# A fused retention and MLP kernel on one core: step inputs in three transfers, y1 stores from ScalarE's queue

## The chip, the core and the metric

The kernel runs on one core of one Trainium2 chip. The metric is device time in microseconds of one execution. A core has five engines that run their own queues in order: TensorE (PE in the profile, PEld for its weight loads), VectorE (DVE), ScalarE (ACT), GpSimd (POOL) and SyncE (SP). In this kernel SyncE only issues DMA transfers; ScalarE issues three at the start. The queue that issues a transfer is named SPq or ACTq.

## What is computed

Three stages follow each other over 3072 tokens: a retention layer (8 heads, head size 64, 4 batches of 768 positions, a state that decays by gamma per position), a first MLP (512 to 1024 to 512, with h * softmax(h) and a layer norm between) and a second MLP (512 to 2048 to 512, with h * cos(h) between).

```python
for t in range(S):
    state = gamma[None, :, None, None] * state + np.einsum('bhd,bhe->bhde', k[:, :, t], v[:, :, t])
    y[:, :, t] = scale * np.einsum('bhd,bhde->bhe', q[:, :, t], state)
...
h = x @ w_in
solu = h * softmax(h)
ln = (solu - mu) / np.sqrt(var + 1e-06) * g_ln
x = ln @ w_out
...
h = x @ w_in
return ((h * np.cos(h)) @ w_out).astype(np.float32)
```

## The kernel before

**Retention in steps.** The positions are cut into chunks of 64. Two batches and all heads go together, so there are 24 steps, two runs of 12. load_step(n) (L83) loads a step's inputs, 1 MB: kt (k by head dimension, 256 KB, two buffers), X (q, two halves of 64 partitions), W (v, two halves of 64 partitions) and kn (k by position, 256 KB); X, W and kn have three buffers. That is six transfers (L91 to L98), all from SyncE. att_prep (L216) lets ScalarE scale kn in place (L223). att_scores multiplies kt and X on TensorE (L230, L231), and VectorE masks the product into the free halves of X (L248). att_state multiplies kn and W into the running state (L241), and ScalarE copies it into the free halves of the next step's W (L255, L256). att_out multiplies W and X to the step's y (L287), and VectorE scales it (L290). attend() (L457) does one round of it: it loads step n+2, prepares step n+1, computes the scores of n+1 and the state and output of n.

**First MLP.** mm1 (L315) multiplies with w1, norm (L318) is softmax and norm over VectorE, ScalarE and GpSimd, transp (L341) transposes the result on TensorE (L351) and splits it into a high part lth (ScalarE, L354) and a rest ltl (VectorE, L355), two buffers of tr. mm2 (L359) multiplies with w_out1; after two halves ScalarE copies the sum to ys (L372, one buffer), and SyncE stores it to y1d in DRAM (L373), 24 stores of 256 KB.

**Weights.** They come as 64-bit floats. load_w (L142) loads a raw tile of 512 KB (L155) into one of three buffers and converts it on ScalarE (L158) and VectorE (L161 to L167) to wt, two buffers. For the tiles that there is no room for yet, keep (L188) stores the converted tile of 256 KB to DRAM (L191), 28 of them; load_kept (L193) fetches them later, two at a time. The list wq (L442) holds all weight tiles, and weights(n) takes the next ones between the other work.

**Second MLP.** load_y (L376) reads y1d back, up (L385) and down (L409) are its two products (L393, L418).

**Order.** TensorE runs in the order of the program text (manual_schedule, L54). The order of every other queue, SyncE's among them, is drawn up by a planner that plays the program through on a timeline of its own (schedule_with_timeline_sim, L663); only single operations are held to program order. Each queue then runs in that order, and an instruction that waits holds up those behind it.

Of the kernel before, what the change touches and what calls it, by code (L numbers as in the profile page):

```python
# [11 lines left out]
F32 = mybir.dt.float32  # L12
# [35 lines left out]


@with_exitstack  # L50
def body(ctx: ExitStack, tc: tile.TileContext, qx, kt, kn, vn, c_sc, c_mg,
         w_in1, w_out1, gln, w_in2, w_out2, out):
    nc = tc.nc
    pe_order = tc.manual_schedule(engines={mybir.EngineType.PE})  # L54
# [28 lines left out]
    def load_step(n):  # L83
        bp, i = steps[n]
        d = {}
        d["kt"] = pa.tile([128, 8, C], F32, tag="kt", name="kt", bufs=2)
        d["X"] = pa.tile([128, 2, 8, C], F32, tag="X", name="X")
        d["kn"] = pa.tile([128, NHP, 2 * D], F32, tag="kn", name="kn")
        d["W"] = pa.tile([128, 2, 8, D], F32, tag="W", name="W")
        d["mg"] = pa.tile([128, 2, NHP, C], F32, tag="mg", name="mg", bufs=2)  # L90
        nc.sync.dma_start(out=d["kt"], in_=kt[bp, i].rearrange("p (j s) -> p j s", s=C))  # L91
        src = qx[bp, i].rearrange("p (j s) -> p j s", s=C)
        nc.sync.dma_start(out=d["X"][64:128, 0], in_=src[64:128])
        nc.sync.dma_start(out=d["X"][0:64, 1], in_=src[0:64])
        src = vn[bp, i].rearrange("p (j s) -> p j s", s=D)
        nc.sync.dma_start(out=d["W"][0:64, 0], in_=src[0:64])
        nc.sync.dma_start(out=d["W"][64:128, 1], in_=src[64:128])
        nc.sync.dma_start(out=d["kn"], in_=kn[bp, i].rearrange("p (j s) -> p j s", s=2 * D))  # L98
        if i == 0:
            nc.gpsimd.memset(d["W"][64:128, 0], 0.0)  # L100
            nc.gpsimd.memset(d["W"][0:64, 1], 0.0)
        st[n] = d

    load_step(0)
# [37 lines left out]
    def load_w(src, apart=False):  # L142
        seq[0] += 1
        if early:
            raw = early.pop(0)
            src = None
            t = p_boot.tile([128, 512], I32, tag="wt", name="wt", bufs=4)
        elif "lt" not in p2 and seq[0] % 2:
            raw = p2["boot"].tile([128, 512, 2], I32, tag="raw", name="raw", bufs=3)
            t = p2["boot"].tile([128, 512], I32, tag="wt", name="wt", bufs=2)  # L150
        else:
            raw = stg.tile([128, 512, 2], I32, tag="raw", name="raw", bufs=3)
            t = stg.tile([128, 512], I32, tag="wt", name="wt")
# [31 lines left out]
    w2h, w2l = {}, {}  # L185
    kept = {}

    def keep(kind, c, e, k, src):  # L188
        if k == 0:
            kept[kind, c, e] = dram.tile([128, 2, 512], F32, name=f"kept_{kind}_{c}_{e}")  # L190
        nc.sync.dma_start(out=kept[kind, c, e][:, k], in_=load_w(src))  # L191

    def load_kept(what, hi, lo):  # L193
        t = stg.tile([128, 2, 512], F32, tag="raw", name="raw", bufs=3)
# [30 lines left out]
    def score_pair(n, j):  # L225
        d = st[n]
        if j == 0:
            d["sc"] = psa.tile([128, 8, C], F32, tag="sc", name="sc")
        sc = d["sc"]
        nc.tensor.matmul(out=sc[0:64, j], lhsT=d["kt"][64:128, j], rhs=d["X"][64:128, 0, j], start=True, stop=True)  # L230
        nc.tensor.matmul(out=sc[64:128, j], lhsT=d["kt"][0:64, j], rhs=d["X"][0:64, 1, j], start=True, stop=True)  # L231

    def state_pair(n, j):
        i = steps[n][1]
        d = st[n]
        if i == 0 and j == 0:
            s_ps[0] = psa.tile([128, 8, D], F32, tag="S", name="S")
        sp = s_ps[0]
        k3 = d["kn"].rearrange("p a (b d) -> p (a b) d", b=2)
        for r, par in ((slice(0, 64), 0), (slice(64, 128), 1)):  # L240
            nc.tensor.matmul(out=sp[r, j], lhsT=k3[r, j], rhs=d["W"][r, par, j],  # L241
                             start=(i == 0 and j == 0), stop=(i == NI - 2 and j == 7), skip_group_check=True)

    def score_mask(n):
        d = st[n]
        sc = d["sc"]
        for r, par in ((slice(0, 64), 0), (slice(64, 128), 1)):
            nc.vector.tensor_tensor(  # L248
                out=d["X"][r, par].rearrange("p (a b) t -> p a b t", b=2),
                in0=sc[r].rearrange("p (a b) t -> p a b t", b=2),  # L250
                in1=d["mg"][r, 0].unsqueeze(2).to_broadcast([64, NHP, 2, C]), op=ALU.mult)

    def state_copy(n):
        nd, sp = st[n + 1], s_ps[0]
        nc.scalar.activation(out=nd["W"][64:128, 0], in_=sp[0:64], func=AF.Copy)  # L255
        nc.scalar.activation(out=nd["W"][0:64, 1], in_=sp[64:128], func=AF.Copy)  # L256

    def att_scores(n):
        for j in range(8):
# [22 lines left out]
    def att_out(n):  # L282
        d = st[n]
        y = psa.tile([128, 8, C], F32, tag="y", name="y")
        for j in range(8):
            for par in range(2):
                nc.tensor.matmul(out=y[64 * par:64 * par + 64, j], lhsT=d["W"][:, par, j], rhs=d["X"][:, par, j],  # L287
                                 start=True, stop=True)
# [70 lines left out]
    def mm2(g, p, e):  # L359
        if e == 0:  # L360
            y1s[g] = p2["pst"].tile([128, 2, 256], F32, tag="y1", name="y1")
        y1 = y1s[g]
        ds = slice((2 * p + e) * 128, (2 * p + e + 1) * 128)
        m = 0
        for j in range(K1):
            lh, ll = lt[g][j // 2]
            for w, a in ((o1[0], lh), (o1[1], lh), (o1[0], ll)):
                nc.tensor.matmul(out=y1[:, e], lhsT=w[:, j, ds], rhs=a[:, j % 2], start=(m == 0), stop=(m == 3 * K1 - 1))  # L368
                m += 1
        if e == 1:  # L370
            ys = moe.tile([128, 2, 256], F32, tag="ys", name="ys", bufs=1)
            nc.scalar.activation(out=ys, in_=y1, func=AF.Copy)  # L372
            nc.sync.dma_start(out=y1d[g // 2][:, 2 * p:2 * p + 2, (g % 2) * 256:(g % 2) * 256 + 256], in_=ys)  # L373


    def load_y(n):  # L376
        yh = p2["sb"].tile([128, KD, 512], F32R, tag="yh", name="yh")
        yl = p2["sb"].tile([128, KD, 512], F32R, tag="yl", name="yl")
        for k in range(KD):
            t = p2["sb"].tile([128, 512], F32, tag="yt", name="yt", bufs=2)  # L380
            nc.sync.dma_start(out=t, in_=y1d[n][:, k])
            split(yh[:, k], yl[:, k], t)
        p2["y", n] = (yh, yl)
# [153 lines left out]
    for s in range(EARLY, NG):  # L537
# [104 lines left out]


# [23 lines left out]
```

## Time and profile before

| | |
|---|---|
| median of 3 runs | 931.36 us (929.67 to 933.35) |
| span of the profiled execution | 932.8 us |
| TensorE busy | 893.4 us, 96% |
| VectorE busy | 622.7 us, 67% |
| ScalarE busy | 455.5 us, 49% |
| DMA, SyncE's queue | 83.91 MB, 30.0% of 16 engines |
| TensorE's mean granted clock | 0.985 |

The profiled execution's span runs from its first to its last instruction; its own time has no other entry, and it lies within the three runs. Up to 380 us the retention steps, the first MLP and the conversion of weights run side by side; behind that is the second MLP alone. In the page's 40 slices of 23.3 us, the busy tenths show the three parts of the first stage:

```profile
PE   4787999989899999999999999999999999999997
DVE  6899887587667754566766655756575665656654
PEclk7999899989999999999999999999999999999999
DMA  9986354565547422133012002000300030001001
```

A digit is the busy share of a slice in tenths, 9 is 90% or more; PEclk is the granted clock of TensorE in tenths of full speed, DMA the mean busy share of 16 DMA engines.

### The profile page before, as it was taken

Reading aid. Unit: us, or ns where it says so; the run is one execution under the profiler, and the core shown is the slowest. Engines: PE = TensorE matmul, PEld = TensorE weight load, DVE = VectorE, ACT = ScalarE, POOL = GpSimd, SP = SyncE. Lnnn points to the kernel's source line nnn. Section 1 sums busy time; section 2 is a strip of 40 time slices with the busy share of each in tenths; the row PEclk is TensorE's granted clock in tenths of the full one; section 3 lists DMA queues with packets and bytes.
Section 4 is the critical chain, followed back from the end, with each engine's and each line's share of the span. In section 5 each row is a group of like instructions: output and inputs, shape, how many; then the busy total and the mean of one; then the engine's idle time right before and its main releaser. Section 6 shows DMA issues by size and latency. Waiting matters only on the chain.

```text
span 932.8 us, 16044 instructions
## 1 busy us (share of the span) xinstructions
PE 893.4 (96%) x6464; PEld 765.1 (82%) x6464; DVE 622.7 (67%) x1090; ACT 455.5 (49%) x768; POOL 48.0 (5%) x60
## 2 busy tenths in 40 slices
PE   4787999989899999999999999999999999999997
PEld 4676889879799989998888888888888888888886
DVE  6899887587667754566766655756575665656654
ACT  4677666556656555554534333433443343344332
POOL 2112100101011000000000000000000000000000
PEclk7999899989999999999999999999999999999999
DMA  9986354565547422133012002000300030001001
GB/s 260 313 252 194 106 158 146 184 204 161 188 131 226 157 93 90 64 108 111 24 35 56 1 1 73 19 0 1 91 1 1 7 84 1 1 24 45 1 1 46
DMA packets 41884, 85.28 MB, mean 91 GB/s; under 512 B 5457, under 2 KB 11729, under 8 KB 41809
## 3 DMA queue, kind: packets, MB, share of 16 engines
q1 hardware_dynamic: 41376, 83.91, 30.0%
q8 instruction: 51, 0.84, 0.4%
q10 hardware_dynamic: 432, 0.34, 0.1%
q14 instruction: 25, 0.20, 0.1%
HBM read 64.30 MB, written 19.92 MB: 90 GB/s over the span
## 4 chain that ended last, share of the span: by engine, by line
PE 84%; DVE 6%; DMA 5%; ACT 2%; issue 2%; SPq 1%; POOL 0%; DVEq 0%; ACTq 0%
PE h L393 28%; PE acc L418 28%; PE y L368 13%; PE h L315 10%; DMA kn<-kn_dram 3%; PE tr L351 2%; PE y L287 2%; DMA W<-vn_dram 1%; PE sc L230 1%; DVE X L248 1%; DVE wt L164 1%; DVE wt L161 1%; ACT kn L223 1%; ACT junk L328 1%; DVE wt L162 0%
## 5 line engine op out<-in xcount | busy, mean ns | idle before, releaser
L393 PE MATMUL h<-yh,w2h 128*128 128x512 f32 x384 | 149.6, 390 | 0.0
L393 PE MATMUL h<-yl,w2h 128*128 128x512 f32 x384 | 149.4, 389 | 0.0
L393 PE MATMUL h<-yh,w2l 128*128 128x512 f32 x384 | 149.4, 389 | 0.0
L418 PE MATMUL acc<-o2h,gh 128*128 128x512 f32 x384 | 149.4, 389 | 0.0
L418 PE MATMUL acc<-o2h,gl 128*128 128x512 f32 x384 | 149.4, 389 | 0.0
L418 PE MATMUL acc<-o2l,gh 128*128 128x512 f32 x384 | 149.4, 389 | 0.0
L404 ACT ACTIVATE r<-r,hp 128x512 f32<-128x512 f32 x96 | 69.5, 724 | 144.5 <-DVE r L403 144.5
L368 PE MATMUL y<-lth,o1h 128*128 128x256 f32 x384 | 110.2, 287 | 0.0
L368 PE MATMUL y<-ltl,o1h 128*128 128x256 f32 x384 | 108.8, 283 | 0.0
L368 PE MATMUL y<-lth,o1l 128*128 128x256 f32 x384 | 108.6, 283 | 0.0
L401 DVE SCALAR_TENSOR_TENSOR r<-ki,h 128x512 f32<-128x512 int32 x96 | 66.0, 687 | 62.9 <-ACT ki L400 61.9
L405 DVE TENSOR_TENSOR r<-r,h 128x512 f32<-128x512 f32 x96 | 66.0, 687 | 61.6 <-ACT r L404 61.6
L128 DVE TENSOR_TENSOR gl<-r,gh 128x512 fp32r<-128x512 f32 x96 | 66.3, 691 | 45.9 <-ACT gh L125 45.4
L400 ACT ACTIVATE ki<-h 128x512 int32<-128x512 f32 x96 | 57.3, 597 | 74.7 <-PE h L393 74.1
L125 ACT ACTIVATE gh<-r 128x512 fp32r<-128x512 f32 x96 | 60.7, 632 | 65.4 <-DVE r L405 65.4
L393 PEld LDWEIGHTS h<-yh,w2h 128*128 128x128 f32 x384 | 72.1, 188 | 14.9
L418 PEld LDWEIGHTS acc<-o2h,gl 128*128 128x128 f32 x384 | 72.1, 188 | 15.0
L393 PEld LDWEIGHTS h<-yl,w2h 128*128 128x128 f32 x384 | 72.1, 188 | 15.0
L418 PEld LDWEIGHTS acc<-o2l,gh 128*128 128x128 f32 x384 | 72.1, 188 | 14.9
L418 PEld LDWEIGHTS acc<-o2h,gh 128*128 128x128 f32 x384 | 72.0, 188 | 14.9
L393 PEld LDWEIGHTS h<-yh,w2l 128*128 128x128 f32 x384 | 72.1, 188 | 14.8
L315 PE MATMUL h<-w1h,xh 128*128 128x512 f32 x192 | 77.9, 406 | 0.0
(77 smaller groups left out, 1554.3 us busy)
## 6 DMA issues: line engine op xcount, KB each, us to landing
raw<-w_in_dram SPq DMA_DIRECT2D x24, 512.0 KB, 4.4
raw<-w_out_dram SPq DMA_DIRECT2D x24, 512.0 KB, 4.8
kt<-kt_dram SPq DMA_DIRECT2D x24, 256.0 KB, 4.9
X<-qx_dram SPq DMA_DIRECT2D x48, 128.0 KB, 5.0
W<-vn_dram SPq DMA_DIRECT2D x48, 128.0 KB, 4.6
kn<-kn_dram SPq DMA_DIRECT2D x24, 256.0 KB, 5.1
y1d<-ys SPq DMA_DIRECT2D x24, 256.0 KB, 2.1
yt<-y1d SPq DMA_DIRECT2D x24, 256.0 KB, 2.9
```

The costliest lines, as they stand in the source:

```text
L125: op = nc.scalar.activation(out=hi, in_=src if head is None else head, func=AF.Copy)
L128: nc.vector.tensor_tensor(out=lo, in0=src, in1=hi.bitcast(F32), op=ALU.subtract)
L287: nc.tensor.matmul(out=y[64 * par:64 * par + 64, j], lhsT=d["W"][:, par, j], rhs=d["X"][:, par, j], start=True, stop=True)
L315: nc.tensor.matmul(out=h[:, c], lhsT=a[:, k], rhs=w[:, k, cs], start=(k + m == 0), stop=(k == KD - 1 and m == 2))
L351: nc.tensor.transpose(out=tr[:, e, t * 128:(t + 1) * 128], in_=lns[2 * g + t].rearrange("p c f -> p (c f)")[:, j * 128:(j + 1) * 128], ide ...
L368: nc.tensor.matmul(out=y1[:, e], lhsT=w[:, j, ds], rhs=a[:, j % 2], start=(m == 0), stop=(m == 3 * K1 - 1))
L393: nc.tensor.matmul(out=h, lhsT=w[:, k, cs], rhs=a[:, k], start=(m == 0), stop=(m == 3 * KD - 1))
L400: nc.scalar.activation(out=ki, in_=h, func=AF.Identity, scale=INV2PI, bias=0.25)
L401: nc.vector.scalar_tensor_tensor(out=r, in0=ki, scalar=-C1, in1=h, op0=ALU.mult, op1=ALU.add)
L404: nc.scalar.activation(out=r, in_=r, func=AF.Sin, bias=hp[:, 0:1])
L405: nc.vector.tensor_tensor(out=r, in0=r, in1=h, op=ALU.mult)
L418: nc.tensor.matmul(out=acc, lhsT=a[:, ts_], rhs=w, start=(j == 0 and m == 0), stop=(j == K2 - 1 and m == 2))
```

## The change

Three things are changed.

1. A step's inputs come in three transfers instead of six, for all steps but the first. k by dimension and k by position lie side by side in DRAM and in one tile ks of 512 KB (three buffers), loaded at once, 4 KB for each of 128 partitions. q and v are laid out crosswise in one tile xw: partitions 64 to 127 get their half of q and their half of v in one transfer, partitions 0 to 63 theirs in another, 4 KB for each of 64 partitions. The tiles that the engines see are the same. k goes first, the two crosswise halves behind it. Step 0 keeps six transfers in the old order.
2. The store of ys to y1d is issued by ScalarE instead of SyncE.
3. keep() no longer stores a tile right behind its own conversion; it holds it and stores it when the next tile is kept, in front of that tile's load. The last is stored behind the loop.

```diff
-        d["kt"] = pa.tile([128, 8, C], F32, tag="kt", name="kt", bufs=2)
-        d["X"] = pa.tile([128, 2, 8, C], F32, tag="X", name="X")
-        d["kn"] = pa.tile([128, NHP, 2 * D], F32, tag="kn", name="kn")
-        d["W"] = pa.tile([128, 2, 8, D], F32, tag="W", name="W")
+        ks = pa.tile([128, 2, 8, C], F32, tag="ks", name="ks")
+        xw = pa.tile([128, 4, 8, C], F32, tag="xw", name="xw")
+        d["kt"] = ks[:, 0]
+        d["kn"] = ks[:, 1].rearrange("p (a b) d -> p a (b d)", b=2)
+        d["X"] = (xw[:, 0], xw[:, 3])
+        d["W"] = (xw[:, 2], xw[:, 1])
...
-        nc.sync.dma_start(out=d["kt"], in_=kt[bp, i].rearrange("p (j s) -> p j s", s=C))
-        src = qx[bp, i].rearrange("p (j s) -> p j s", s=C)
-        nc.sync.dma_start(out=d["X"][64:128, 0], in_=src[64:128])
-        nc.sync.dma_start(out=d["X"][0:64, 1], in_=src[0:64])
-        src = vn[bp, i].rearrange("p (j s) -> p j s", s=D)
-        nc.sync.dma_start(out=d["W"][0:64, 0], in_=src[0:64])
-        nc.sync.dma_start(out=d["W"][64:128, 1], in_=src[64:128])
-        nc.sync.dma_start(out=d["kn"], in_=kn[bp, i].rearrange("p (j s) -> p j s", s=2 * D))
+        ksrc = kk[bp, i].rearrange("p (u j s) -> p u j s", u=2, s=C)
+        xsrc = qv[bp, i].rearrange("p (u j s) -> p u j s", u=2, s=C)
+        if n == 0:
+            nc.sync.dma_start(out=ks[:, 0], in_=ksrc[:, 0])
...
+            nc.sync.dma_start(out=ks[:, 1], in_=ksrc[:, 1])
+        else:
+            nc.sync.dma_start(out=ks, in_=ksrc)
+            nc.sync.dma_start(out=xw[64:128, 0:2], in_=xsrc[64:128])
+            nc.sync.dma_start(out=xw[0:64, 2:4], in_=xsrc[0:64])
...
+    held = []
+
+    def flush_kept():
+        while held:
+            dst, t = held.pop(0)
+            nc.sync.dma_start(out=dst, in_=t)
+
     def keep(kind, c, e, k, src):
         if k == 0:
             kept[kind, c, e] = dram.tile([128, 2, 512], F32, name=f"kept_{kind}_{c}_{e}")
-        nc.sync.dma_start(out=kept[kind, c, e][:, k], in_=load_w(src))
+        flush_kept()
+        held.append((kept[kind, c, e][:, k], load_w(src)))
...
             nc.scalar.activation(out=ys, in_=y1, func=AF.Copy)
-            nc.sync.dma_start(out=y1d[g // 2][:, 2 * p:2 * p + 2, (g % 2) * 256:(g % 2) * 256 + 256], in_=ys)
+            nc.scalar.dma_start(out=y1d[g // 2][:, 2 * p:2 * p + 2, (g % 2) * 256:(g % 2) * 256 + 256], in_=ys)
...
     weights(len(wq))
+    flush_kept()
     load_y(0)
```

## Rows read from the trace of the kernel before

**Rows 1.** The page's head: busy us, share of the span, instructions.
```profile
PE 893.4 (96%) x6464; PEld 765.1 (82%) x6464; DVE 622.7 (67%) x1090; ACT 455.5 (49%) x768; POOL 48.0 (5%) x60
```

**Rows 2.** Stretches: length, busy us by engine (PE, PEld, DVE, ACT, POOL), clock, DMA, GB/s.
```profile
20.00:40.00 20.00, 14.87 (x211) 12.45 (x212) 16.83 (x30) 13.70 (x31) 1.78 (x2) 0.81 1.05 313
40.00:60.00 20.00, 19.22 (x331) 16.06 (x329) 18.65 (x33) 15.20 (x31) 3.91 (x4) 1.00 0.88 257
180.00:200.00 20.00, 15.77 (x172) 13.57 (x171) 13.58 (x28) 12.80 (x24) 1.72 (x3) 0.83 0.47 147
240.00:260.00 20.00, 17.64 (x201) 15.69 (x200) 13.77 (x28) 12.63 (x24) 2.01 (x4) 1.00 0.47 149
420.00:900.00 480.00, 480.00 (x2120) 397.44 (x2119) 301.65 (x486) 192.68 (x310) 0.00 (x0) 1.00 0.10 28
```

**Rows 3.** TensorE's waits, 185 to 200 and 240 to 256: total us, times, longest.
```profile
PE tr L351 <- DVE ltl L355: 4.1, 1, 4.1
...
PE tr L351 <- DVE ltl L355: 2.4, 2, 1.8
```

**Rows 4.** ScalarE's timeline at both stalls: start, length, operation [idle before <-releaser].
```profile
181.22 1.28 ACT L223 ACTIVATE kn<-kn,cs 128x128 f32<-128x128 f32 x4 [5.68 <-DMA kn<-kn_dram]
...
186.55 0.60 ACT L372 ACTIVATE ys<-y 128x512 f32<-128x512 f32 x1
...
187.61 1.07 ACT L354 ACTIVATE lth<-tr 128x512 fp32r<-128x512 f32 x2
...
241.03 1.28 ACT L223 ACTIVATE kn<-kn,cs 128x128 f32<-128x128 f32 x4 [3.67 <-DMA kn<-kn_dram]
```

**Rows 5.** ScalarE's waits from 100 to 380 us, the longest group.
```profile
ACT kn L223 <- DMA kn<-kn_dram: 24.4, 9, 5.7
```

**Rows 6.** SyncE's queue, timeline of its issues from 172 us.
```profile
172.38 0.39 SPq L155 DMA_DIRECT2D raw<-w_out_dram  x1
172.86 0.38 SPq L91 DMA_DIRECT2D kt<-kt_dram  x1
173.33 0.42 SPq L98 DMA_DIRECT2D kn<-kn_dram  x1
```

**Rows 7.** TensorE's timeline, the last state products before those issues.
```profile
172.35 0.23 PE L241 MATMUL S<-W,kn 64*64 64x64 f32 x2
```

**Rows 8.** The chain that ended last: start, length, what.
```profile
173.33 7.86 DMA kn<-kn_dram
```

**Rows 9.** Waits of the whole run: SyncE's queue, then ScalarE for raw weights.
```profile
SPq L373 <- ACT ys L372: 110.4, 20, 10.9
SPq L191 <- DVE wt L167: 74.9, 24, 9.0
...
ACT wt L158 <- DMA raw<-w_in_dram: 2.9, 4, 0.9
```

**Rows 10.** Stretches of one microsecond while kn was in flight.
```profile
180.00:181.00 1.00, 1.00 (x6) 0.83 (x5) 0.00 (x0) 0.00 (x0) 0.00 (x0) 1.00 0.06 23
```

**Rows 11.** TensorE's timeline in the start, the scores of step 1.
```profile
16.57 0.44 PE L230 MATMUL sc<-X,kt 64*64 64x64 f32 x2 [5.38 <-DMA X<-qx_dram]
```

**Rows 12.** ScalarE's timeline in the start, kn of steps 1 and 2.
```profile
19.74 1.28 ACT L223 ACTIVATE kn<-kn,cs 128x128 f32<-128x128 f32 x4 [3.40 <-DMA kn<-kn_dram]
...
23.57 1.28 ACT L223 ACTIVATE kn<-kn,cs 128x128 f32<-128x128 f32 x4 [2.03 <-DMA kn<-kn_dram]
```

**Rows 13.** VectorE's timeline in the start: step 1's mask, a split behind w1h.
```profile
19.72 1.40 DVE L248 TENSOR_TENSOR X<-sc,mg 64x512 f32<-64x512 f32 x2
...
26.63 0.69 DVE L128 TENSOR_TENSOR w1l<-raw,w1h 128x512 fp32r<-128x512 f32 x1 [2.98 <-ACT w1h L125]
```

**Rows 14.** Stretches of the start: mostly step loads, then raw weights.
```profile
13.00:22.00 9.00, 4.21 (x64) 3.85 (x64) 8.79 (x16) 4.21 (x10) 1.35 (x1) 0.55 1.07 241
23.00:26.00 3.00, 3.00 (x39) 2.35 (x38) 0.65 (x2) 2.39 (x7) 0.00 (x0) 0.82 1.03 421
```

**Rows 15.** ScalarE's queue, timeline of an issue at the start.
```profile
0.73 0.41 ACTq L108 DMA_DIRECT2D mg<-c_mg_dram  x1
```

More of the change, by code (lines that the diff above doesn't have):

```diff
@@ L50, in body @@
 @with_exitstack
-def body(ctx: ExitStack, tc: tile.TileContext, qx, kt, kn, vn, c_sc, c_mg,
+def body(ctx: ExitStack, tc: tile.TileContext, kk, qv, c_sc, c_mg,
          w_in1, w_out1, gln, w_in2, w_out2, out):
@@ L85, in load_step @@
         d = {}
-        d["kt"] = pa.tile([128, 8, C], F32, tag="kt", name="kt", bufs=2)
-        d["X"] = pa.tile([128, 2, 8, C], F32, tag="X", name="X")
-        d["kn"] = pa.tile([128, NHP, 2 * D], F32, tag="kn", name="kn")
-        d["W"] = pa.tile([128, 2, 8, D], F32, tag="W", name="W")
-        d["mg"] = pa.tile([128, 2, NHP, C], F32, tag="mg", name="mg", bufs=2)
-        nc.sync.dma_start(out=d["kt"], in_=kt[bp, i].rearrange("p (j s) -> p j s", s=C))
-        src = qx[bp, i].rearrange("p (j s) -> p j s", s=C)
-        nc.sync.dma_start(out=d["X"][64:128, 0], in_=src[64:128])
-        nc.sync.dma_start(out=d["X"][0:64, 1], in_=src[0:64])
-        src = vn[bp, i].rearrange("p (j s) -> p j s", s=D)
-        nc.sync.dma_start(out=d["W"][0:64, 0], in_=src[0:64])
-        nc.sync.dma_start(out=d["W"][64:128, 1], in_=src[64:128])
-        nc.sync.dma_start(out=d["kn"], in_=kn[bp, i].rearrange("p (j s) -> p j s", s=2 * D))
+        ks = pa.tile([128, 2, 8, C], F32, tag="ks", name="ks")
[4 more added lines that the diff above has]
+        d["W"] = (xw[:, 2], xw[:, 1])
+        d["mg"] = pa.tile([128, 2, NHP, C], F32, tag="mg", name="mg", bufs=2)
+        ksrc = kk[bp, i].rearrange("p (u j s) -> p u j s", u=2, s=C)
+        xsrc = qv[bp, i].rearrange("p (u j s) -> p u j s", u=2, s=C)
+        if n == 0:
+            nc.sync.dma_start(out=ks[:, 0], in_=ksrc[:, 0])
+            nc.sync.dma_start(out=xw[64:128, 0], in_=xsrc[64:128, 0])
+            nc.sync.dma_start(out=xw[0:64, 3], in_=xsrc[0:64, 1])
+            nc.sync.dma_start(out=xw[0:64, 2], in_=xsrc[0:64, 0])
+            nc.sync.dma_start(out=xw[64:128, 1], in_=xsrc[64:128, 1])
+            nc.sync.dma_start(out=ks[:, 1], in_=ksrc[:, 1])
[3 more added lines that the diff above has]
+            nc.sync.dma_start(out=xw[0:64, 2:4], in_=xsrc[0:64])
         if i == 0:
-            nc.gpsimd.memset(d["W"][64:128, 0], 0.0)
-            nc.gpsimd.memset(d["W"][0:64, 1], 0.0)
+            nc.gpsimd.memset(d["W"][0][64:128], 0.0)
+            nc.gpsimd.memset(d["W"][1][0:64], 0.0)
         st[n] = d
@@ L229, in score_pair @@
         sc = d["sc"]
-        nc.tensor.matmul(out=sc[0:64, j], lhsT=d["kt"][64:128, j], rhs=d["X"][64:128, 0, j], start=True, stop=True)
-        nc.tensor.matmul(out=sc[64:128, j], lhsT=d["kt"][0:64, j], rhs=d["X"][0:64, 1, j], start=True, stop=True)
+        nc.tensor.matmul(out=sc[0:64, j], lhsT=d["kt"][64:128, j], rhs=d["X"][0][64:128, j], start=True, stop=True)
+        nc.tensor.matmul(out=sc[64:128, j], lhsT=d["kt"][0:64, j], rhs=d["X"][1][0:64, j], start=True, stop=True)
     def state_pair(n, j):
@@ L240, in state_pair @@
         for r, par in ((slice(0, 64), 0), (slice(64, 128), 1)):
-            nc.tensor.matmul(out=sp[r, j], lhsT=k3[r, j], rhs=d["W"][r, par, j],
+            nc.tensor.matmul(out=sp[r, j], lhsT=k3[r, j], rhs=d["W"][par][r, j],
                              start=(i == 0 and j == 0), stop=(i == NI - 2 and j == 7), skip_group_check=True)
@@ L248, in score_mask @@
             nc.vector.tensor_tensor(
-                out=d["X"][r, par].rearrange("p (a b) t -> p a b t", b=2),
+                out=d["X"][par][r].rearrange("p (a b) t -> p a b t", b=2),
                 in0=sc[r].rearrange("p (a b) t -> p a b t", b=2),
@@ L254, in state_copy @@
         nd, sp = st[n + 1], s_ps[0]
-        nc.scalar.activation(out=nd["W"][64:128, 0], in_=sp[0:64], func=AF.Copy)
-        nc.scalar.activation(out=nd["W"][0:64, 1], in_=sp[64:128], func=AF.Copy)
+        nc.scalar.activation(out=nd["W"][0][64:128], in_=sp[0:64], func=AF.Copy)
+        nc.scalar.activation(out=nd["W"][1][0:64], in_=sp[64:128], func=AF.Copy)
     def att_scores(n):
@@ L286, in att_out @@
             for par in range(2):
-                nc.tensor.matmul(out=y[64 * par:64 * par + 64, j], lhsT=d["W"][:, par, j], rhs=d["X"][:, par, j],
+                nc.tensor.matmul(out=y[64 * par:64 * par + 64, j], lhsT=d["W"][par][:, j], rhs=d["X"][par][:, j],
                                  start=True, stop=True)
@@ L641, in _by_s, with _crossed @@
     return np.ascontiguousarray(a.reshape(NB2, NI, 128, 8 * D))
+def _crossed(x, w):
+    return np.ascontiguousarray(np.concatenate([
+        np.concatenate([w[:, :, :64], x[:, :, :64]], axis=-1),
+        np.concatenate([x[:, :, 64:], w[:, :, 64:]], axis=-1)], axis=2))
 def kernel(q, k, v, moe_w_in, moe_w_out, moe_g_ln, moe2_w_in, moe2_w_out):
@@ L649 @@
     ins = [
-        ("qx", _by_d(q, True)), ("kt", _by_d(k, True)), ("kn", _by_s(k)), ("vn", _by_s(v)),
+        ("kk", np.concatenate([_by_d(k, True), _by_s(k)], axis=-1)), ("qv", _crossed(_by_d(q, True), _by_s(v))),
         ("c_sc", cs), ("c_mg", mg),
```

## The prediction

> **What bounds the kernel now.** I read the head of the page first, then the stretches, then the waits of the engine that is short, then its releasers. The page says that TensorE is 96% busy [rows 1]. That is an average over two halves, and the stretches take it apart [rows 2]: from 420 to 900 us TensorE is busy all of the time, with DMA at a share of 0.10. Nothing that this change touches lies on that path, so some 550 us of the span can't answer to it. Before 380 us there are three kinds of stretch. Up to 40 us the DMA engines are full (a share of 1.05). From 40 us VectorE is (18.65 of 20 us), and in the table of slices it stays so until about 100. After that TensorE is the bound, except for two stalls, in the stretches from 180 (15.77 of 20 us busy, mean clock 0.83) and from 240 (17.64 of 20).
>
> Those two stalls are what a change of transfers could win back. TensorE's waits give their size, 4.1 and 2.4 us, both of the transposes (L351) for VectorE's ltl (L355) [rows 3]. ltl follows ScalarE's lth, and ScalarE's timeline says why that is late: at 181.22 it had stood 5.68 us for the load of kn, at 241.03 it had stood 3.67 [rows 4]. Then it works off what was queued, ys among it, and only at 187.61 come the two lth. So TensorE loses 1.6 us less than ScalarE waited the first time (5.68 - 4.1) and 1.3 the second (3.67 - 2.4): that is the slack. The whole window from 100 to 380 us holds nine such waits, 24.4 us in all [rows 5]; the other seven cost TensorE next to nothing. And the kn that was waited for was issued at 173.33, right behind the kt of 172.86 [rows 6], and took 7.86 us to land [rows 8].
>
> Was the issue late, because SyncE's queue stood behind a store? SyncE does stand: 110.4 us for ys in front of y1d stores and 74.9 us for converted tiles in front of kept stores [rows 9]. But of raw weights, queued behind the same stores, ScalarE waited for 2.9 us at L158 in the whole run [rows 9]. And kt and kn go out right behind the work that frees their buffers: the last state product of that step starts at 172.35 and takes 0.23 us [rows 7], kt follows at 172.86. So SyncE's long waits are mostly idle time of an engine that is not the bound. What is late is the landing. In the microsecond from 180 the transfers were down to a DMA share of 0.06 and 23 GB/s [rows 10]: a few packets that lagged, not a backlog.
>
> **Part 1, fewer transfers.** 23 of 24 steps go from six issues to three, so 69 are removed from SyncE. At the 0.38 and 0.42 us of kt and kn [rows 6] that is some 28 us of a queue with slack, counted at nothing; its cover is the long waits of SyncE above. The bytes stay 1 MB a step.
>
> For the two stalls: kn's bytes now go out with kt's, at kt's place, 0.47 us earlier (173.33 - 172.86). Its 256 KB stood behind kt's 256 KB and now stand beside them, so the last byte comes no sooner than that. Gain 0.47 us a stall, and 0 if the lagging packets decide.
>
> For the start: step 1's scores need kt and both X halves. They stood first to third of the six, and TensorE had waited 5.38 us when they came at 16.57 [rows 11]; kn was last, and ScalarE got it at 19.74 after 3.40 us [rows 12]. Now k comes first and X last: the scores start when the whole step is in, about 19.7, so 3.2 us later, and the score mask, which VectorE reached at 19.72 [rows 13], comes 3 us later. Against that, kn of steps 1 and 2 comes sooner. At the 241 GB/s of this stretch [rows 14] half a step is 0.524 MB / 241 = 2.2 us, so step 2's kn lands near 21.4 instead of 23.57, and ScalarE's 2.03 us of standing [rows 12] goes. That standing held w1h back, for which VectorE was idle 2.98 us at 26.63 [rows 13]. Between the two on ScalarE stand the state copies, though, and these need the state product that follows the late scores. One idle stretch takes the place of the other. I count the start at 0, between -3.0 (all of VectorE's 2.98 goes, as it is the bound afterwards) and +3.2 (the scores' delay goes through).
>
> Rows of 4 KB instead of 2 KB could add speed. The raw weights, 4 KB rows on 128 partitions, moved at 421 GB/s; the stretch of step loads at 241 [rows 14]. Half of a step's bytes are X and W, 64 partitions a transfer, and these stay so. The rows can't part row length from halves. I leave the speed at 0, and the -3.0 holds it, since VectorE has that much idle time there to give back. The Trainium skill, "DMA: Bandwidth & Descriptors", Rules for kernel authors, says that two transfers to disjoint partition halves serialize on the same engines, and to use one of 128 partitions instead; by it the crosswise halves keep the larger loss, and with halves at half of 421 a step would take 1.25 us for k and 2.5 for the rest, 3.7 us against 4.35 at 241, 0.6 us a step as an estimate.
>
> **Part 2, y1d stores from ScalarE's queue.** The 24 issues leave SyncE (nothing, as above) and go behind ys on ScalarE, 18 of them before 380 us. An issue there took 0.41 us [rows 15]. It must wait for its own ys to be complete, so an overlap of operations goes too; 0.1 us is my estimate of it, since lth, two of them, took 1.07 us together where one ys took 0.60 [rows 4]: about 0.5 us a store. Behind it at 187 us stand the two lth that TensorE waits for, so in the two stalls all of it counts: +1.0 us. The other 16 lie under a slack like the 1.3 to 1.6 us above and cost nothing; without that cover they cost up to 16 x 0.5 = 8 us.
>
> **Part 3, kept stores one tile late.** Each of the 28 stores goes in front of the next tile's load, when its tile is long converted, so the 74.9 us of SyncE's standing shrink. No load behind was late, so nothing comes of it directly. What may come: raw loads go out earlier and are not in front of a step load, as the 512 KB of 172.38 are [rows 6]. At 421 GB/s that is 1.25 us; between 0 (three raw buffers hold the load back anyway) and 1.25 I take the middle, 0.6 us a stall. On the other side a wt buffer is freed later. There are two, so the conversion two tiles on would have to come before the store has landed; no such wait shows now, and I count 0, with the 8 us above as the far end for it too.
>
> **Sum.** Start 0; two stalls at -0.47 - 0.6 + 0.5 = -0.57 each, -1.1 in all. The profiled span of 932.8 us is 1.4 above the median and within the runs. Taken off the median: 931.4 - 1.1 = 930.3 us. On the span it would be 931.7.
>
> **The rivals.**
> A, both stalls go (faster). kn lands 4.1 and 2.4 us sooner, because one transfer lags less than two, or because the planner, which sees one longer transfer, puts the scaling of kn (L223) later in ScalarE's order. For it: by the code the state product that uses the scaled kn stands a whole attend() behind the scaling, so a later place would do. Against: nothing in the change addresses lagging packets. It gives 4.1 + 2.4 = 6.5 us, and of the low clock, 0.17 of 20 us in the first stretch, at most 3.4: up to 9.9 us, and 921.5 us. Half of it would be 926.
>
> B, the stores on ScalarE come through (slower). Its place is ScalarE's order between ys and lth; its price 0.5 us a store, all 18 make 9, half of them 4.5; it decides when ScalarE's slack before the transposes is under 0.5 us in most tiles. For it: lth stands behind ys in the same queue. Against: seven waits for kn, 15 us of ScalarE's time (24.4 - 5.68 - 3.67), cost TensorE almost nothing. With the start at +3.2 and half of the stores it gives 931.4 + 3.2 + 4.5 = 939.
>
> C, the change does not do what it says. SyncE's order is the planner's; it may put a late store where the early one stood, and the load of k where kn's was. For it: kt and kn go out together already. Then the time is that of before, 931.4.
>
> **How the numbers follow.** My forecast gets 0.43, A 0.26, B 0.19, C 0.12. The predicted time is 930.3 us. Of A I leave out its far end and keep down to 922; of B I keep up to 938: some 0.1 stay outside on each side. A measurement of this kernel can tell about 0.5% (4.7 us) from no change. Faster by more: A without its weakest form, 0.22, and 0.07 from my forecast where the start gives all 3.0 and the stalls a little more, 0.29. Slower by more: B without its weakest form 0.15, and 0.05 from the forecast with the start at +3.2 and some stores uncovered, 0.20. Within: 0.51.
>
> **What would show it.** Right: from 420 us on nothing moves; step 1's scores start near 19.7; ScalarE's waits for k in the window from 100 to 380 us stay near 20 us, with transposes late twice by 3 to 4 and 2 us; SyncE's waits at kept and y1d lines vanish without TensorE gaining. A is right if TensorE's waits for ltl are gone and the clock is full from 100 us. B is right if new waits of TensorE for lth or ltl stand right behind y1d issues of ScalarE. I am wrong if the start moves by more than 4 us, which would mean that row length or the order of the loads, not VectorE's work, sets it, or if ScalarE waits for raw weights or wt buffers.

## The result and the profile after

The changed kernel takes 944.09 us, the median of four runs (941.51 to 947.67), against 931.48 for the kernel before in the same comparison (929.67 to 933.35): a ratio of 1.0143, with an interval of 1.0113 to 1.0173. It is slower by about 13 us; 930.3 was predicted, with 938 as the upper end. The profiled execution is the fastest of the four (941.51 us, a span of 939.7), so its trace shows 6.9 us of the loss against the span of 932.8 before.

Where these 6.9 us come in is read from the stretches and from one tile. First the page's head of the changed kernel, columns as in [rows 1]:

```profile
PE 895.3 (95%) x6464; PEld 765.0 (81%) x6464; DVE 622.1 (66%) x1090; ACT 455.6 (48%) x768; POOL 47.1 (5%) x60
```

Then its stretches, columns as in [rows 2]:

```profile
180.00:200.00 20.00, 15.82 (x169) 13.93 (x168) 12.10 (x26) 11.00 (x20) 1.59 (x2) 0.83 0.49 152
240.00:260.00 20.00, 17.24 (x199) 15.39 (x198) 13.43 (x29) 12.60 (x24) 1.59 (x2) 1.00 0.53 171
420.00:900.00 480.00, 480.00 (x2134) 398.04 (x2133) 303.08 (x487) 194.39 (x312) 0.00 (x0) 1.00 0.11 31
```

Between 180 and 200 us TensorE is idle for as long as in [rows 2], between 240 and 260 for 0.4 us longer, and from 420 us on TensorE is busy throughout, as it was. The tile ys, one for each store of y1, dates the loss (ScalarE's operations on ys between 113 and 349 us: count, durations, first and last start). The kernel before:

```profile
L372 ACT ACTIVATE ys<-y x17: 584/599/602, 113.1 to 342.1; 128x512 f32<-128x512 f32 x17
```

The changed kernel:

```profile
L387 ACT ACTIVATE ys<-y x17: 577/598/601, 113.4 to 348.8; 128x512 f32<-128x512 f32 x17
```

The first starts 0.3 us later, the seventeenth 6.7. So nearly all of the loss in this trace comes between 113 and 349 us, bit by bit: 6.4 us over 16 intervals, 0.40 us each on average. What TensorE waits for (100 to 420 us: total, times, longest) was one group in the kernel before:

```profile
PE tr L351 <- DVE ltl L355: 7.6, 5, 4.1
```

In the changed kernel it is more often, and a second group is there:

```profile
PE tr L366 <- DVE ltl L370: 10.8, 8, 4.2
PE h L330 <- DVE sm L344: 1.3, 2, 0.8
```

These waits grew by 4.5 us in all. ScalarE's timeline at the first stall shows what now stands between ys and the lth for which ltl and the transposes wait (start, length, operation, idle before it):

```profile
183.43 1.28 ACT L238 ACTIVATE ks<-ks,cs 128x128 f32<-128x128 f32 x4 [4.21 <-DMA ks<-kk_dram]
...
188.77 0.60 ACT L387 ACTIVATE ys<-y 128x512 f32<-128x512 f32 x1
189.40 0.37 ACTq L388 DMA_DIRECT2D y1d<-ys  x1
189.86 0.69 ACT L165 ACTIVATE wt<-raw 128x512 f32<-128x512 f32 x1 [0.50 <-ACT ys L387]
190.43 1.08 ACT L369 ACTIVATE lth<-tr 128x512 fp32r<-128x512 f32 x2
```

From ys to lth it is 1.66 us; in [rows 4] it was 1.06 (187.61 - 186.55). The store has put in 0.60 us: it waits for ys to be complete, issues for 0.37, and the conversion behind it no longer overlaps ys.

The start was late in the way that the steps said, by less. The scores of step 1 wait 7.60 instead of 5.38 us [rows 11] and start 2.3 us later, where 3.2 had been worked out; the mask starts at 22.07 instead of 19.72 [rows 13]. These are TensorE's and VectorE's timelines in the changed kernel:

```profile
18.88 0.44 PE L245 MATMUL sc<-xw,ks 64*64 64x64 f32 x2 [7.60 <-DMA xw<-qv_dram]
...
22.07 1.41 DVE L263 TENSOR_TENSOR xw<-sc,mg 64x512 f32<-64x512 f32 x2 [0.20 <-PE sc L246]
```

And the stretch that is mostly step loads:

```profile
13.00:22.00 9.00, 2.45 (x44) 2.29 (x46) 8.76 (x16) 5.19 (x11) 1.36 (x1) 0.54 1.04 273
```

That stretch moved 273 GB/s where it had moved 241 [rows 14]. It mixes step loads with weights, and rows became longer as transfers became fewer, so the gain can't be given to one of them. The Trainium skill, "DMA: Bandwidth & Descriptors", Rules for kernel authors, prefers one transfer of 128 partitions to two of disjoint halves. No run here tests that: q and v come in halves in both kernels, k in neither.

### The profile page after: what moved, and what is told of

Read it like the earlier page. It is cut to its first block, busy times and chain, and to the rows that moved or that the text cites. A ratio compares the mean times of both kernels' runs of the same rounds, so it can differ in the third digit from the quotient of the medians.

```text
span 939.7 us, 15921 instructions
## 1 busy us (share of the span) xinstructions
PE 895.3 (95%) x6464; PEld 765.0 (81%) x6464; DVE 622.1 (66%) x1090; ACT 455.6 (48%) x768; POOL 47.1 (5%) x60
## 4 chain that ended last, share of the span: by engine, by line
PE 73%; DVE 9%; DMA 8%; ACT 5%; issue 3%; POOL 1%; SPq 0%; ACTq 0%; DVEq 0%
PE acc L433 28%; PE h L408 28%; PE y L383 7%; PE h L330 6%; DMA ks<-kk_dram 5%; DMA raw<-w_in_dram 2%; PE tr L366 2%; DVE wt L171 1%; ACT wt L165 1%; PE y L302 1%; PE sc L245 1%; ACT junk L343 1%; ACT ks L238 1%; DVE ltl L370 1%; DVE wt L174 1%
```

## The experiments

The candidates were the price of the stores on ScalarE (rival B), part 1's start, and part 3.

**The parts alone.** Each kernel is the kernel before with one part of the change, or two.

e1_p1_only:
```diff
+            nc.sync.dma_start(out=ks, in_=ksrc)
+            nc.sync.dma_start(out=xw[64:128, 0:2], in_=xsrc[64:128])
+            nc.sync.dma_start(out=xw[0:64, 2:4], in_=xsrc[0:64])
```


> Part 1 alone: a step's inputs in three transfers, y1d stores back on SyncE, kept stores at once. Theory L (the loads do it: q and v come last, the step is whole only with its last transfer, and the planner orders ScalarE and VectorE anew around it): 940 us or more, that is at least two thirds of the 12.6 us that the whole change lost. Theory S (the y1 stores on ScalarE's queue do it): within 3 us of before, 928 to 935. Theory T (each part gives a third): 934 to 937.

938.35 us (935.91 to 939.99), ratio 1.0090 (1.0062 to 1.0119).

e2_p2_only:
```diff
-            nc.sync.dma_start(out=y1d[g // 2][:, 2 * p:2 * p + 2, (g % 2) * 256:(g % 2) * 256 + 256], in_=ys)
+            nc.scalar.dma_start(out=y1d[g // 2][:, 2 * p:2 * p + 2, (g % 2) * 256:(g % 2) * 256 + 256], in_=ys)
```


> Part 2 alone: y1d stores from ScalarE's queue, six transfers a step, kept stores at once. Theory S (each of 18 stores before 380 us holds ScalarE for 0.5 us in front of lth, and TensorE's transposes wait for it): 938 to 944, with new waits of TensorE for ltl right behind the issues. Theory L: within 3 us of before. Theory T: 934 to 937.

942.0 us (939.98 to 944.22), ratio 1.0139 (1.0114 to 1.0163).

e3_p3_only:
```diff
+        flush_kept()
+        held.append((kept[kind, c, e][:, k], load_w(src)))
```


> Part 3 alone: kept stores one tile late. The order of ScalarE's and of VectorE's instructions is that of before, line for line; only SyncE's differs. Theory W (a store held back frees its wt buffer late, and a conversion waits for it): 935 us or more, with waits of ScalarE's conversion L158 or of VectorE behind it. Theories L and S: within 2 us of before, 929 to 933.

932.02 us (928.79 to 933.34), ratio 1.0017 (1.0001 to 1.0033). ScalarE and VectorE run in the order of before.

e4_p1_p3:
```diff
-            nc.scalar.dma_start(out=y1d[g // 2][:, 2 * p:2 * p + 2, (g % 2) * 256:(g % 2) * 256 + 256], in_=ys)
+            nc.sync.dma_start(out=y1d[g // 2][:, 2 * p:2 * p + 2, (g % 2) * 256:(g % 2) * 256 + 256], in_=ys)
```
(against the changed kernel)


> The changed kernel with the y1d stores back on SyncE: parts 1 and 3. Theory S: back to before, 929 to 935. Theory L: as slow as the changed kernel, 940 to 945. Theory I (parts 1 and 2 lose only together, since the planner's order of VectorE changes far more under both than under either): within 3 us of before here, and also with part 1 or part 2 alone.

940.6 us (934.14 to 946.26), ratio 1.0121 (1.0068 to 1.0174).

Part 3 is worth next to nothing, part 2 alone loses what the whole loses, and part 1 alone two thirds of it. They don't add up (8 + 12 against 13), so they seem to lose by the same waits.

**What in parts 1 and 2.** e5 and e6 split part 1 into its start and the rest; e7 takes the stores off SyncE without putting them on ScalarE; e8 leaves the stores on SyncE and gives ScalarE the time alone.

e5_p1_start_old, part 1 with steps 0 to 4 in six transfers (against e1):
```diff
-        if n == 0:
+        if n < 5:
```


> Part 1 alone, but steps 0 to 4 keep six transfers in the old order (into the same tiles); steps 5 to 23 come in three. Theory LS (part 1 loses in the start, where the DMA engines are full and the scores wait for the whole step): back to before, 928 to 933, and the first ys near 113 us. Theory LA (it loses all along, through later landings of k): 936 us or more, like part 1 alone.

936.29 us (933.77 to 941.41), ratio 1.0054 (1.0033 to 1.0076).

e6_p1_start_only, part 1 with only steps 1 to 4 in three (against e1):
```diff
-        if n == 0:
+        if n == 0 or n > 4:
```


> The counterpart: part 1 alone, but only steps 1 to 4 come in three transfers, steps 5 to 23 in six. Theory LS: as slow as part 1 alone, 935 to 941, the first ys 1 to 5 us later than before. Theory LA: within 3 us of before.

936.09 us (932.76 to 940.02), ratio 1.0049 (1.0029 to 1.0069). The start alone and the rest alone lose almost 5 us each, all of part 1 loses 8.

e7_y1d_gpsimd:
```diff
-            nc.sync.dma_start(out=y1d[g // 2][:, 2 * p:2 * p + 2, (g % 2) * 256:(g % 2) * 256 + 256], in_=ys)
+            nc.gpsimd.dma_start(out=y1d[g // 2][:, 2 * p:2 * p + 2, (g % 2) * 256:(g % 2) * 256 + 256], in_=ys)
```


> y1d stores from GpSimd's queue instead of ScalarE's, all else as before. The order of ScalarE's and VectorE's instructions is that of before, line for line, and SyncE's queue is free of the stores as with part 2. Theory S (part 2 loses by ScalarE's time): 928 to 934. Theory F (part 2 loses because the freed SyncE queue moves loads and stores together): 938 or more.

933.64 us (928.96 to 938.13), ratio 1.0017 (0.9995 to 1.0040).

e8_ys_twice:
```diff
             nc.scalar.activation(out=ys, in_=y1, func=AF.Copy)
+            nc.scalar.activation(out=ys, in_=y1, func=AF.Copy)
             nc.sync.dma_start(out=y1d[g // 2][:, 2 * p:2 * p + 2, (g % 2) * 256:(g % 2) * 256 + 256], in_=ys)
```


> y1d stores stay on SyncE; ScalarE copies y1 to ys twice, the second time over the first, so about 0.5 us a tile more of ScalarE at the place where part 2 has its issue. VectorE's order is that of part 2 alone, ScalarE's nearly. Theory S: as slow as part 2 alone, 937 to 943. Theory F: within 3 us of before.

943.96 us (939.29 to 945.55), ratio 1.0115 (1.0078 to 1.0152).

So part 2 costs ScalarE's time, not a queue: half a microsecond of another operation behind ys loses as much. And SyncE, freed of 110.4 us of waits [rows 9], gives nothing back. The Trainium skill, "Trainium Kernel Development and Optimization", Key Constraints, says that issuing from several engines saves only issue time; here what it saves on SyncE is worth nothing (e7), and ScalarE has to pay for it.

For part 1's rest the trace shows a move. In e3, with six transfers, ScalarE's timeline has the norm's square (junk) ahead of the scaling of k (kn):

```profile
194.88 1.15 ACT L336 ACTIVATE junk<-u,sm 128x1024 bf16<-128x1024 f32 x1 [1.50 <-DVE sm L335]
...
197.37 1.28 ACT L231 ACTIVATE kn<-kn,cs 128x128 f32<-128x128 f32 x4 [1.25 <-DMA kn<-kn_dram]
198.57 1.25 ACT L344 ACTIVATE u<-u,sm 128x1024 f32<-128x1024 f32 x1
199.84 0.60 ACT L380 ACTIVATE ys<-y 128x512 f32<-128x512 f32 x1
```

In e5's timeline the scaling (of ks, the tile that now holds k) stands ahead of the square, which then waits for k as well (from the ys before to this one it takes 18.0 us, in e3 15.9):

```profile
198.26 1.28 ACT L230 ACTIVATE ks<-ks,cs 128x128 f32<-128x128 f32 x4 [3.26 <-DMA ks<-kk_dram]
199.45 1.13 ACT L335 ACTIVATE junk<-u,sm 128x1024 bf16<-128x1024 f32 x1
...
202.16 1.24 ACT L343 ACTIVATE u<-u,sm 128x1024 f32<-128x1024 f32 x1 [1.49 <-DVE sm L342]
203.43 0.60 ACT L379 ACTIVATE ys<-y 128x512 f32<-128x512 f32 x1
```

That the planner does so because one transfer looks earlier to it is argued, not shown. Nor is this move shown to be e5's whole loss. The next stall has it too (18.4 against 16.5 us), but from the first ys to the last the two traces differ by 0.9 us only (303.1 against 302.2), and 3.5 us lie before the first ys (115.7 against 112.2), whose start also varies by 3 us among the six-transfer kernels (e2 112.1, e7 115.1).

**k's scaling held back.** The second theory (K) put everything on the time that ScalarE stands waiting for k: parts 1 and 2 only made that wait longer. Its test keeps the scaling in program order, behind the evictions lth.

e9_pin_base, the kernel before with:
```diff
-                nc.scalar.activation(out=d["kn"][:, a], in_=d["kn"][:, a], func=AF.Copy, scale=cs[:, 2, i, a:a + 1])
+                op = nc.scalar.activation(out=d["kn"][:, a], in_=d["kn"][:, a], func=AF.Copy, scale=cs[:, 2, i, a:a + 1])
+                if n > 12:
+                    tc.keep_in_program_order(op)
```


> The kernel before, with one constraint: from step 13 on, the scaling of k stands in program order on ScalarE, so that the planner cannot put it ahead of the tile's other ScalarE work; while k is still landing, ScalarE goes on with the transposes' evictions. Theory K (what parts 1 and 2 lose after the start goes through ScalarE standing for k, ahead of work that TensorE needs): the stalls near 190 and 250 us, 4.1 and 2.4 us in the trace of before, go, and the full clock holds from 100 us on, so 921 to 929 us. If ScalarE's wait for k decided nothing: 931 us. The scaling may also come late for its own users; then it is slower than before, up to 940 us.

923.75 us (923.25 to 924.23), ratio 0.9925 (0.9906 to 0.9944). It beats both kernels.

e10_pin_p2, the edit of e2 on top:
```diff
-            nc.sync.dma_start(out=y1d[g // 2][:, 2 * p:2 * p + 2, (g % 2) * 256:(g % 2) * 256 + 256], in_=ys)
+            nc.scalar.dma_start(out=y1d[g // 2][:, 2 * p:2 * p + 2, (g % 2) * 256:(g % 2) * 256 + 256], in_=ys)
```


> e9_pin_base with part 2 alone on top (the stores of y1 issued by ScalarE). Theory K: ScalarE's extra 0.5 us at a store only hurts because k's transfer then starts behind two others and ScalarE stands for it; with that wait out of the way the kernel is within 3 us of e9_pin_base. Rival S0: the 0.5 us of each store comes through by itself, so e9_pin_base + 9 to 12 us.

934.87 us (933.64 to 937.01), ratio 1.0046 (1.0028 to 1.0063).

e11_pin_after, the changed kernel with the edit of e9:
```diff
+                if n > 12:
+                    tc.keep_in_program_order(op)
```


> The whole change with the same constraint. Theory K: what is left of its price is part 1's start, so e9_pin_base + about 4.5 us. Rival S0: the stores come through as well, e9_pin_base + 12 us or more.

935.05 us (933.33 to 938.34), ratio 1.0053 (1.0032 to 1.0073): no more above e9 than e10 is, 11.3 us.

e12_pin_p1late, e5 with the edit of e9:
```diff
+                if n > 12:
+                    tc.keep_in_program_order(op)
```


> e5_p1_start_old (steps 0 to 4 in six transfers, the rest in three) with the same constraint. Theory K: part 1's later loss was the scaling of k put ahead of the norm's square, which the constraint forbids, so within 3 us of e9_pin_base. If the loss comes from the three transfers themselves: e9_pin_base + 5 us.

926.14 us (922.04 to 929.49), ratio 0.9951 (0.9932 to 0.9969).

Theory K holds for the stalls, it fits part 1's rest (e12 is 2.4 us above e9, which the scatter hardly tells from nothing), and it falls for part 2: with no wait for k left, the stores still cost 11.1 us (e10 against e9). The stretch from 110 to 420 us says it too, columns as in [rows 2]. For e9:

```profile
110.00:420.00 310.00, 309.86 (x2994) 281.11 (x2992) 218.07 (x420) 182.84 (x308) 25.77 (x31) 1.00 0.48 152
```

For e10:

```profile
110.00:420.00 310.00, 303.98 (x2955) 272.32 (x2955) 210.31 (x412) 179.88 (x303) 26.99 (x32) 1.00 0.46 146
```

And TensorE's waits in that stretch of e10 (total, times, longest):

```profile
PE tr L353 <- DVE ltl L357: 4.6, 12, 0.7
PE h L317 <- DVE sm L331: 1.1, 4, 0.4
```

No single stall is left in e10, but TensorE waits twelve times for ltl, at most 0.7 us each. The tile ys gives the pace (operations on ys between 148 and 330 us: count, durations, first and last start). In e9:

```profile
L374 ACT ACTIVATE ys<-y x13: 576/598/601, 149.4 to 316.2; 128x512 f32<-128x512 f32 x13
```

In e10:

```profile
L374 ACT ACTIVATE ys<-y x13: 577/598/602, 154.1 to 328.5; 128x512 f32<-128x512 f32 x13
```

Twelve intervals take 166.8 us in e9, 174.4 in e10: 0.63 us a store on average. All 24 stores (timelines of ys over the whole run) start between 111.8 and 406.4 us in e9, between 114.3 and 419.0 in e10: from the last of these thirteen (316.2 and 328.5) to the very last it is 90.2 and 90.5 us. So the late stores cost next to nothing, and the price is paid before 330 us.

**The place of the store.** One chain in these traces accounts for it: tr has two buffers, the third transpose waits for ltl, ltl for lth, and lth stands on ScalarE behind ys. The timeline of e9, on ScalarE, VectorE and TensorE:

```profile
236.45 0.60 ACT L374 ACTIVATE ys<-y 128x512 f32<-128x512 f32 x1
236.95 0.68 ACT L158 ACTIVATE wt<-raw 128x512 f32<-128x512 f32 x1
237.52 1.08 ACT L356 ACTIVATE lth<-tr 128x512 fp32r<-128x512 f32 x2
...
238.46 0.68 DVE L357 TENSOR_TENSOR ltl<-tr,lth 128x512 fp32r<-128x512 f32 x1
...
240.06 1.04 PE L353 MATMUL tr<-ident,u 128*128 128x128 f32 x8
```

The same place in e10's timeline:

```profile
245.01 0.60 ACT L374 ACTIVATE ys<-y 128x512 f32<-128x512 f32 x1
245.64 0.37 ACTq L375 DMA_DIRECT2D y1d<-ys  x1
246.05 0.66 ACT L158 ACTIVATE wt<-raw 128x512 f32<-128x512 f32 x1 [0.44 <-ACT ys L374]
246.62 1.07 ACT L356 ACTIVATE lth<-tr 128x512 fp32r<-128x512 f32 x2
...
247.23 0.69 DVE L357 TENSOR_TENSOR ltl<-tr,lth 128x512 fp32r<-128x512 f32 x1
...
247.98 0.66 PE L353 MATMUL tr<-ident,u 128*128 128x128 f32 x4 [0.67 <-DVE ltl L357]
```

lth comes 1.61 instead of 1.07 us after ys, and the transposes wait 0.67 us for it. Theory P says that the place between ys and lth is the price; rival T, that ScalarE's total time is. The test moves the same issues on the same queue: 12 stand behind the lth of the next transposes, 12 at least one operation (a conversion, or the norm) behind ys.

e13_pin_p2late, against e10:
```diff
-            nc.scalar.dma_start(out=y1d[g // 2][:, 2 * p:2 * p + 2, (g % 2) * 256:(g % 2) * 256 + 256], in_=ys)
+            late.append((y1d[g // 2][:, 2 * p:2 * p + 2, (g % 2) * 256:(g % 2) * 256 + 256], ys))
...
+    def flush_y1():
+        while late:
+            dst, t = late.pop(0)
+            tc.keep_in_program_order(nc.scalar.dma_start(out=dst, in_=t))
...
         transp(g, 3)
+        flush_y1()
...
         first(2 * s + 1, 0)
+        flush_y1()
```


> e10_pin_p2 with its 24 stores still on ScalarE's queue, but issued later: instead of directly behind the eviction ys they stand, in program order, behind the evictions lth of the next transposes (12 of them) or behind the next half tile's norm work (the other 12). Theory P (a store costs because of its place, between ys and the lth that TensorE's next transposes wait for): within 3 us of e9_pin_base, 924 to 927 us, and no wait of TensorE for ltl. Rival T (ScalarE's total time decides, wherever the 0.5 us stands): as e10_pin_p2, 935 us.

923.43 us (922.25 to 926.41), ratio 0.9933 (0.9910 to 0.9956). The 11 us are gone, with as many issues on ScalarE. In the stretch from 110 us TensorE is busy without a gap:

```profile
110.00:420.00 310.00, 310.00 (x2999) 281.66 (x2998) 218.31 (x422) 184.22 (x310) 26.52 (x31) 1.00 0.48 151
```

ScalarE's timeline in e13 shows that more has changed than the place:

```profile
269.39 0.37 ACTq L365 DMA_DIRECT2D y1d<-ys  x1
269.47 0.59 ACT L356 ACTIVATE lth<-tr 128x512 fp32r<-128x512 f32 x1
269.95 1.27 ACT L223 ACTIVATE kn<-kn,cs 128x128 f32<-128x128 f32 x4
```

Here the issue runs beside lth, and the operation behind it starts 0.11 us before lth ends, as if no issue were there. ys has long been complete, so nothing waits for it: from 100 to 420 us, ScalarE's operations other than ys wait for ys ten times in e10 (4.7 us), once in e13 (0.4 us). So the half microsecond was not moved, it is gone, and e13 can't tell the place from the wait for ys. That half a microsecond of ScalarE's time at the first place is enough is shown by e8, which has no issue there and loses as much as e2. What the same time would cost behind lth was not run, so rival T is open in part.

e14_pin_p1, e1 with the edit of e9:
```diff
+                if n > 12:
+                    tc.keep_in_program_order(op)
```


> Part 1 alone, all steps in three transfers, with the scaling of k in program order from step 13 on. e12_pin_p1late, which differs only in steps 0 to 4, was 2.4 us above e9_pin_base. If part 1's start price is as without the constraint (e1_p1_only was 938.35 us, e5_p1_start_old 936.29): e12_pin_p1late + 2 to 5 us, so 928 to 931 us. If the start costs nothing: 926 us.

925.41 us (923.09 to 926.22), ratio 0.9930 (0.9906 to 0.9954): the start costs nothing that can be told.

e15_pin_afterlate, the changed kernel with the edits of e9 and e13:
```diff
+                    tc.keep_in_program_order(op)
...
+            tc.keep_in_program_order(nc.scalar.dma_start(out=dst, in_=t))
```


> The whole change with both constraints, k's scaling in program order and the stores of y1 issued as in e13_pin_p2late. Theory P: only part 1's start is left, so as e14_pin_p1, within 3 us. Rival T: as e11_pin_after, 935 us.

923.48 us (922.90 to 923.64), ratio 0.9922 (0.9899 to 0.9945).

**The place alone, with k not held back.**

e16_p2_place, e2 with the stores at that place:
```diff
-            nc.scalar.dma_start(out=y1d[g // 2][:, 2 * p:2 * p + 2, (g % 2) * 256:(g % 2) * 256 + 256], in_=ys)
+            late.append((y1d[g // 2][:, 2 * p:2 * p + 2, (g % 2) * 256:(g % 2) * 256 + 256], ys))
```


> e2_p2_only (942.0 us) with its 24 stores issued by ScalarE at the later place of e13_pin_p2late, and nothing held back for k. ScalarE and VectorE then do their work in exactly the order of the kernel before, with 24 issues put in between. Theory P (the place between ys and lth is what a store costs): 930 to 934 us, as before. If the stores cost ScalarE's time wherever they stand: 939 to 942 us.

934.45 us (928.95 to 936.20), ratio 1.0016 (0.9991 to 1.0041). By the ratio 1.5 us are left of e2's 13; the median lies just above what P expected.

e17_after_place, the changed kernel likewise:
```diff
-            nc.scalar.dma_start(out=y1d[g // 2][:, 2 * p:2 * p + 2, (g % 2) * 256:(g % 2) * 256 + 256], in_=ys)
+            late.append((y1d[g // 2][:, 2 * p:2 * p + 2, (g % 2) * 256:(g % 2) * 256 + 256], ys))
```


> The whole change with its stores at that later place and nothing held back for k; ScalarE's order is that of e4_p1_p3 with 24 issues put in between. Theory P: as e4_p1_p3 (940.6 us, its runs from 934 to 946), so 934 to 941 us. Otherwise as the changed kernel, 944 us, or above.

939.69 us (937.52 to 944.63), ratio 1.0092 (1.0058 to 1.0127): what is left is part 1's loss, as in e1 and e4.

Put together, medians in us:

| stores of y1, step inputs | k's scaling free | k's scaling held back |
|---|---|---|
| SyncE, six transfers | 931.5 (before) | 923.75 (e9) |
| SyncE, three | 938.35 (e1) | 925.4 (e14) |
| ScalarE behind ys, six | 942.0 (e2) | 934.9 (e10) |
| ScalarE later, six | 934.45 (e16) | 923.4 (e13) |
| ScalarE behind ys, three, part 3 | 944.1 (after) | 935.05 (e11) |
| ScalarE later, three, part 3 | 939.7 (e17) | 923.5 (e15) |

The times come from several comparisons, in which the kernel before had medians from 930.2 to 931.5. In the right column, stores right behind ys cost 11 to 12 us, everything else at most 2. In the left column, part 1 costs 5 to 8 us where the stores are on SyncE or later, and about 2 on top of stores behind ys.

## Why the prediction was wrong, step by step

**Part 2, "the other 16 lie under a slack and cost nothing".** This is the step that failed. The size of a store was right (0.5 us estimated; from ys to lth it is 0.54 us longer in e10 and 0.60 in the changed kernel), and the far end, 16 x 0.5 = 8 us beside the 1.0 in the stalls, came near what e10 lost (11.1). The count of 18 was low: in the kernel before 20 of the 24 stores start before 380 us. The cover was wrong. I took the 1.3 to 1.6 us by which TensorE lost less than ScalarE had waited [rows 3, 4], and the seven waits for k without a cost [rows 5], for slack at every store. But ScalarE stood for k some 6 us ahead of lth (181.22 against 187.61, [rows 4]); the store stands one conversion ahead of it, and the cover there is two buffers of tr. The slack has to be read between the instruction moved and the next one that TensorE waits for. Rival B had the place, the mechanism and the price of 0.5 us; its "half of them" was still too low, as e10 pays 0.63 us at each of twelve on average.

**Part 1, "gain 0.47 us a stall".** k did come sooner, by about that much: in the changed kernel ScalarE starts on it 6.9 us after the issue of ks (183.43 - 176.54), in e2, where the raw tile goes out as far ahead, 7.3 us after that of kt (182.42 - 175.12, rows below). SyncE's issue in the changed kernel:

```profile
176.54 0.40 SPq L103 DMA_DIRECT2D ks<-kk_dram  x1
```

No time was won by it, and in the rest of the steps about 5 us went (e5). This step took ScalarE's order as given, and the planner moved k's scaling ahead of the norm's square. With the scaling held in program order, part 1 loses 2.4 us or less (e12, e14), so its loss goes through ScalarE standing for k; that the move is all of it is not shown. Rival A had named the planner's order of this scaling, but expected it later, not earlier.

**The start, "0, between -3.0 and +3.2".** Scores and mask were late by 2.3 and 2.4 us, not by 3.2 and 3 (18.88 and 22.07 against 16.57 and 19.72), and in the changed kernel's trace the first ys is only 0.3 us later, as the 0 said. The half rate that the prediction's 0.6 us a step puts on the crosswise halves was a supposition, and no run here shows it. Steps 1 to 4 in three transfers alone cost 4.6 us (e6); with k's scaling held back from step 13 on, they cost nothing that can be told (e14 against e12). So the 4.6 us, more than the +3.2 of the range, need the later waits for k. By what path a start in three transfers makes those worse wasn't settled.

**Part 3, 0.6 us a stall for the raw tile no longer in front.** The late store takes the early one's place, and raw still stands in front of k; rival C was right for this part. The term itself seems to have been too small, though the time did not fall with it. SyncE's issues ahead of the first stall in e2, and ScalarE's scaling of k behind them (timelines):

```profile
174.64 0.38 SPq L155 DMA_DIRECT2D raw<-w_out_dram  x1
175.12 0.41 SPq L91 DMA_DIRECT2D kt<-kt_dram  x1
175.62 0.38 SPq L98 DMA_DIRECT2D kn<-kn_dram  x1
...
182.42 1.28 ACT L223 ACTIVATE kn<-kn,cs 128x128 f32<-128x128 f32 x4 [4.62 <-DMA kn<-kn_dram]
```

The same in e3:

```profile
171.61 0.38 SPq L155 DMA_DIRECT2D raw<-w_out_dram  x1
173.14 0.33 SPq L91 DMA_DIRECT2D kt<-kt_dram  x1
173.57 0.38 SPq L98 DMA_DIRECT2D kn<-kn_dram  x1
...
178.58 1.28 ACT L231 ACTIVATE kn<-kn,cs 128x128 f32<-128x128 f32 x4 [2.83 <-DMA kn<-kn_dram]
```

Where raw goes out 0.48 us ahead of kt, ScalarE starts on k 6.8 us after kn's issue in e2 (182.42 - 175.62) and 7.9 in the kernel before [rows 4, 6]; where it is 1.53 us, 5.0 in e3. So in these single stalls about a microsecond of distance went with two to three, where I had bounded the term at 1.25. In e3 the median stayed that of before all the same.

**SyncE's waits "vanish".** They moved: in the changed kernel the kept line stands 120.2 us instead of the 74.9 of [rows 9].

SyncE's waits there:

```profile
SPq L200 <- DVE wt L174: 120.2, 24, 11.1
```

That they cost nothing was right: in e7 they moved likewise, and the time stayed.

**What was right.** Nothing moved after 420 us. ScalarE's waits for k stayed (27.4 us in nine, against 24.4 [rows 5]). The stalls were worth what rival A said: with k's scaling behind lth, both go, the clock in e9 is 1.00 from 110 to 420 us, and 6.7 us are won, within A's 6.5 to 9.9. The reason given there, that the state product comes a whole attend() later, was the way to it; the change just doesn't go that way.

## What to carry to other kernels

The slack of an engine is not its idle share but the time between the moved instruction and the next one behind it that the bounding engine waits for. Here an issue right behind the operation that makes its data, and in front of a PSUM eviction that TensorE needs, cost about 0.6 us a store; the same issue a few operations later cost nothing that can be told. Where a planner orders a queue, look in the new order for what else moved: here one early in-place scaling, waiting for its load ahead of work that was ready, was worth 6.7 us, half of what the change lost. Parts that lose by the same wait don't add up, so measure them both with that wait and without it.

## What the runs showed of the hardware

A store issued by ScalarE right behind the operation that makes its data takes more of the engine than its 0.37 us: the next operation starts 0.44 us (e10) to 0.50 us (changed kernel) after ys has ended, where without the store it starts 0.10 us before ys ends (236.95 against 236.45 + 0.60 in e9). A store whose data has long been complete takes none of it: in e13 the issue of 0.37 us at 269.39 runs beside lth, and the next operation starts 0.11 us before lth ends. And a load of 256 KB, issued behind 768 KB of others that had gone out in the microsecond before, took 6.8 us (e2) to be used; with the 512 KB of the raw tile a microsecond further ahead it took 5.0 us (e3).
